# Polysketch attention and cosine router: queries in the keys' form, routing in pieces, ten early expert blocks

## The chip, the cores and the metric

One Trainium2 chip, one of its cores. The metric is the device time of one execution in microseconds (us). The engines are TensorE (PE in the views; PEld is its weight loads), VectorE (DVE), ScalarE (ACT), GpSimd (POOL) and SyncE (SP, which issues plain DMAs). SBUF is the working memory of 128 partitions; PSUM is where TensorE writes.

## The reference

Polynomial-sketch attention for 4 batches x 4 heads, 1088 positions of 32 numbers, then a router that sends each of 4352 tokens (128 numbers, the four heads side by side) to the best of 8 experts.

```python
phi(x) = outer(S1 @ x, S2 @ x).reshape(64)          # 8 x 8 features of a position
kv, z = sum_s phi(k_s) v_s^T, sum_s phi(k_s)
x = (phi(q) @ kv) / (phi(q) . z + 1e-6)             # 4 heads -> 128 numbers per token
logits = normed(x) @ normed(expert_emb).T / tau
e, g = argmax(logits), softmax(logits)[argmax]
out = g * (relu(x @ w1[e]) @ w2[e])                 # w1[e]: 128 x 1024, w2[e]: 1024 x 128
```

All inputs and the output are float32.

## The kernel before

The batches are handled in two halves (m = 0, 1) of two batches; a half has 17 tiles of 128 positions.

**Keys** (`k_steps`, L256): in groups of four tiles, `tr` transposes the tiles on TensorE, `ab` multiplies them with the block matrix `Sblk` (L270, 96 columns), ScalarE copies one sketch out, VectorE multiplies the two to features `kp` (L276), and `kv` adds up features times values over all tiles in PSUM (L288). At the end the sums go to `kz`, with a mask that keeps each head's own part.

**Queries** (`q_steps`, L311) have features across partitions: `fa` and `fb` multiply the transposed tiles with the expanded sketches `Sa` and `Sb` (L328, up to 512 columns, two passes for each of two head pairs), ScalarE copies one product and VectorE multiplies it with the other (L340). `nd` multiplies with `kz` (L348, weights of 64 columns, one half of the output's partitions at a time), VectorE divides (L354 to L356), `xt` transposes the result, ScalarE sums squares, `logit` multiplies with the embeddings (L372).

**Order.** `k_steps` and `q_steps` are lists of steps that `put` lays on ticks (L555 to L572): keys of m = 0 one group per tick, then keys of m = 1 with queries of m = 0, then queries of m = 1. A scheduler orders the instructions of these stages.

**Routing** (`pick` L379, `gate_tokens` L394, `route_and_run_experts` L413) comes after all logits: one-hot choices, two products that count them and rank them (L418, L419), a scan, slots, gates on all tokens (on GpSimd), one write per half of the gated tokens to the DRAM buffer `x_dram`, then a table from block and row to token, built with products of one-hot rows and columns (L454 to L470). From it come `src_i`, `dst_i` (token to gather, row to scatter) and `exp_i` (expert of each block).

**Expert blocks** (L542): 41 blocks of 128 tokens, in written order on VectorE and TensorE. Block i: `fetch(i + 4)` gathers tokens with an indirect DMA on GpSimd (L497), `up(i)` does 16 passes and a Relu on ScalarE (L522, L523), `turn(i + 1)` transposes the next tokens (L503, L505), `weights(i + 1)` copies the expert's matrices by a number that VectorE loads to a register (L512, L513), `down(i - 1)` does 16 passes, a copy on ScalarE (L531) and an indirect DMA that scatters to the output (L532). TensorE executes its queue in order.

Of the kernel before, what the change touches and what calls it, by code (L numbers as in the profile page):

```python
# [19 lines left out]
P = 128  # L20
# [13 lines left out]
K_GROUPS = ((0, 4), (4, 8), (8, 12), (12, 16), (16, 17))  # L34
Q_GROUPS = ((0, 4), (4, 8), (8, 11), (11, 14), (14, 17))
# [4 lines left out]
DIGIT = 128  # L40
AHEAD = 4
# [8 lines left out]
def kernel(  # L50
# [28 lines left out]
    def ps_acc(i):  # L79
        return psum.tile([P, 512], F32, tag=f"acc{i}", bufs=1, name=f"ps_acc{i}")  # L80
# [6 lines left out]
    def rows_tile(name):  # L87
        return rows_p.tile([P, NC, H, D], F32, tag="rows", name=name)

    def load_q(m):  # L90

        for i in range(2):
            for h in range(H):
                nc.sync.dma_start(
                    q_sb[m][i * HALF:(i + 1) * HALF, :, h],
                    bass.AP(tensor=q.tensor, offset=q.offset + ((2 * m + i) * H + h) * S * D,
                            ap=[[NC * D, HALF], [D, NC], [1, D]]))


    v_sb = [consts.tile([P, 6, NC, D], F32, name=f"v{m}") for m in range(NM)]  # L100

    def load_k(m, i):
        for h in range(H):
            nc.sync.dma_start(
                k_sb[m][:, i * NK:(i + 1) * NK, h],
                bass.AP(tensor=k.tensor, offset=k.offset + ((2 * m + i) * H + h) * S * D,
                        ap=[[NK * D, P], [D, NK], [1, D]]))

    def load_v(m, i):
        for p in range(2):  # L110
            nc.sync.dma_start(
                v_sb[m][:, 3 * p:3 * p + 2, i * NK:(i + 1) * NK],
                bass.AP(tensor=v.tensor, offset=v.offset + ((2 * m + i) * H + 2 * p) * S * D,
                        ap=[[NK * D, P], [S * D, 2], [1, NK * D]]))

    def load_rest(m):
        for i in range(2):
            r = slice(i * HALF, (i + 1) * HALF)
            at = (2 * m + i) * H * S * D + SK * D
            nc.sync.dma_start(k_sb[m][r, NC - 1],  # L120
                              bass.AP(tensor=k.tensor, offset=k.offset + at, ap=[[D, HALF], [S * D, H], [1, D]]))
            for p in range(2):
                nc.sync.dma_start(v_sb[m][r, 3 * p:3 * p + 2, NC - 1],
                                  bass.AP(tensor=v.tensor, offset=v.offset + at + 2 * p * S * D,
                                          ap=[[D, HALF], [S * D, 2], [1, D]]))
# [4 lines left out]
    for m in range(NM):  # L130
        k_sb[m] = rows_tile(f"k{m}")
        for i in range(2):
            load_k(m, i)
            load_v(m, i)
        load_rest(m)
        q_sb[m] = rows_tile(f"q{m}")
# [13 lines left out]
    for m in range(NM):  # L150
        for p in range(2):
            nc.gpsimd.memset(v_sb[m][:, 3 * p + 2], 1.0)

    mask4 = consts.tile([P, H], F32, name="mask4")
    maskh = consts.tile([P, 2], F32, name="maskh")
    for t in (mask4, maskh):
        nc.vector.memset(t, 0.0)
    for h in range(H):
        nc.vector.memset(mask4[h * D:(h + 1) * D, h:h + 1], 1.0)
    for h in range(2):  # L160
        nc.vector.memset(maskh[HALF * h:HALF * (h + 1), h:h + 1], 1.0)
# [40 lines left out]
    nc.gpsimd.memset(half_c, 0.5)
    x_dram = tc.dram_tile([N, DM], F32, name="x_dram")
# [8 lines left out]
    lane = iota([P, P], [[1, P]], 0, 0, "lane")  # L212
    part = iota([P, 1], [[1, 1]], 0, 1, "part")
    first = iota([P, E], [[-1, E]], E, 0, "first")
    start = iota([P, NT], [[P, NT]], 0, 0, "start")
# [7 lines left out]
    tok_d = consts.tile([P, 2, NT], F32, name="tok_d")  # L223
    nc.vector.tensor_copy(tok_d, tok_i[:, 1:])
    digits = [tok_d[:, d] for d in range(2)]
    before = consts.tile([P, P], F32, name="before")
    nc.vector.tensor_scalar(before, lane, part[:, 0:1], None, op0=ALU.is_gt)
    ones = consts.tile([P, P], F32, name="ones")
    nc.vector.memset(ones, 1.0)
    follows = consts.tile([P, E, NT], F32, name="follows")  # L230
    nc.vector.memset(follows, 1.0)
    nc.vector.memset(follows[:, :, 0:1], 0.0)

    enT = consts.tile([P, 96], F32, name="enT")
    nc.vector.memset(enT, 0.0)

    def prep_emb():
# [12 lines left out]
        nc.vector.tensor_copy(enT[:, :E], ps[:, :E])  # L250


    kz = {}
    acc = {}

    def k_steps(m, c0, c1):  # L256
# [3 lines left out]
        def tr():  # L260
            ps = ps_small()
            for j in range(n):
                nc.tensor.transpose(ps[:, j * P:(j + 1) * P], k_sb[m][:, c0 + j].rearrange("p h d -> p (h d)"), ident)
            s["kT"] = work.tile([P, 512], F32, tag="xT", name="kT")
            nc.scalar.copy(s["kT"][:, :n * P], ps[:, :n * P])

        def ab():
            ps = ps_small().rearrange("p (j g r) -> p j g r", j=4, r=2 * R)
            for j in range(n):
                nc.tensor.matmul(ps[:, j, :6], s["kT"][:, j * P:(j + 1) * P], Sblk, start=True, stop=True)  # L270
            b_sb = work.tile([P, 4, H, R], F32, tag="b", name="b_sb")
            nc.scalar.copy(b_sb[:, :n], ps[:, :n, :H, R:])  # L272
            s["kp"] = work.tile([P, 4, H, R, R], F32, tag="kp", name="kp")
            for j in range(n):
                a, b = ps[:, j, :H, :R], b_sb[:, j]
                nc.vector.tensor_mul(s["kp"][:, j],  # L276
                                     bview(a, [list(a.ap[1]), list(a.ap[2]), [0, R]]),
                                     bview(b, [list(b.ap[1]), [0, R], list(b.ap[2])]))

        def kv():  # L280
            if c0 == 0:
                acc[m] = [ps_acc(i)[:, :6 * D].rearrange("p (a n) -> p a n", a=2) for i in range(2)]
            for c in range(c0, c1):
                rest = c == NC - 1
                for i in range(2) if rest else (c // NK,):
                    r = slice(i * HALF, (i + 1) * HALF) if rest else slice(0, P)
                    for p in range(2):
                        nc.tensor.matmul(  # L288
                            acc[m][i][:, p],
                            s["kp"][r, c - c0, 2 * p:2 * p + 2].rearrange("s h i j -> s (h i j)"),  # L290
# [318 lines left out]
```

## Time and profile before

| what | us |
|---|---|
| median of 3 runs (307.32 to 312.07) | 307.79 |
| the profiled execution | 309.62 |
| its span, first to last instruction | 307.8 |
| TensorE busy / its weight loads | 254.5 / 230.3 |
| VectorE, ScalarE, GpSimd busy | 140.1, 86.5, 107.2 |

Times below are from the start of the profiled span. In a view, a line names the kernel's line (L522), the engine, the operation, what it writes and reads, shapes, a count, busy time or mean time, and in brackets or after a bar the idle time before it and what ended that. The granted clock is a share of 2.4 GHz: 1.00, or 0.50 for 1.2 GHz, or a mean of both.

### The profile page before, as it was taken

To read this page: it belongs to the slowest core of one execution; us is meant where nothing else is said; L and a number is where in the kernel's file an instruction comes from. 1 tells how busy PE (TensorE), PEld (TensorE's weight loads), DVE (VectorE), ACT (ScalarE), POOL (GpSimd) and SP (SyncE) were. 2 spreads that over 40 slices of the span, in tenths; PEclk is the share of its full clock that TensorE was granted. 3 is DMA by queue.
4 is the path that set the end of the run, shared out by engine and by line. 5 is a ranking of instruction groups with operands and counts; after the bars stand their busy time and mean duration, and the time that the engine had idled before them with its cause. 6 is when DMAs were issued, how large, how long until landed. Compare 5 with 4: busy or idle time off the path is not lost. (4 is left out here: it accounts for less than half of the span.)

```text
span 307.8 us, 5515 instructions
## 1 busy us (share of the span) xinstructions
PE 254.5 (83%) x2127; PEld 230.3 (75%) x2127; DVE 140.1 (46%) x345; ACT 86.5 (28%) x195; POOL 107.2 (35%) x103
## 2 busy tenths in 40 slices
PE   0987999999799750125999999999999999999960
PEld 0886777776467530114999999999999999999960
DVE  7334254345464448982344444444444444444400
ACT  1121242332245210001133333333333333333320
POOL 4000000000413034017455666555666556632230
PEclk9999799999999955555799999999999999999995
DMA  6999799993003001102111111111111111210000
GB/s 122 167 136 171 146 135 327 336 345 85 0 2 145 1 2 66 79 0 48 30 34 38 34 37 28 36 30 44 37 30 37 34 40 32 36 25 19 15 2 0
DMA packets 51194, 22.59 MB, mean 73 GB/s; under 512 B 38425, under 2 KB 48676, under 8 KB 50912
## 3 DMA queue, kind: packets, MB, share of 16 engines
q1 hardware_dynamic: 48544, 17.31, 24.2%
q0 software_dynamic: 2624, 4.92, 6.2%
q8 instruction: 17, 0.28, 0.4%
q14 instruction: 9, 0.07, 0.1%
HBM read 17.77 MB, written 4.92 MB: 74 GB/s over the span
## 5 line engine op out<-in xcount | busy, mean ns | idle before, releaser
L522 PE MATMUL ps_big<-xTb,w1b 128*128 128x128 f32 x656 | 83.6, 283 | 1.7 <-issue 1.3
L522 PEld LDWEIGHTS ps_big<-xTb,w1b 128*128 128x128 f32 x656 | 79.8, 199 | 2.4 <-issue 1.7
L529 PE MATMUL ps_acc<-w2b,hT 128*128 128x128 f32 x656 | 79.8, 275 | 0.0
L529 PEld LDWEIGHTS ps_acc<-w2b,hT 128*128 128x128 f32 x656 | 76.4, 192 | 0.0
L523 ACT ACTIVATE hT<-ps_big 128x1024 f32<-128x1024 f32 x41 | 42.1, 1027 | 94.6 <-PE ps_big L522 83.6
L497 POOL DMA_INDIRECT xs<-x_dram,src_i x41 | 48.0, 1170 | 39.4 <-PE ps_t L503 21.4
L532 POOL DMA_INDIRECT out_dram<-y,dst_i x41 | 41.4, 1010 | 50.3 <-ACT y L531 48.4
L505 DVE COPY xTb<-ps_t 128x128 f32<-128x128 f32 x41 | 12.0, 292 | 75.0 <-PE ps_t L503 75.0
L512 DVE COPY w1b<-w_sb 128x1024 f32 x41 | 28.5, 694 | 13.5 <-DVE xTb L505 12.1
L399 POOL TENSOR_TENSOR nrm<-ssq,half_c 128x17 f32<-128x17 f32 x2 | 6.2, 3087 | 65.7 <-ACT sq L367 65.7
L513 DVE COPY w2b<-w_sb 128x1024 f32 x41 | 28.5, 694 | 0.0
L340 DVE TENSOR_TENSOR qp<-a_sb,ps_big 128x768 f32<-128x768 f32 (+1 forms) x10 | 10.6, 1055 | 23.4 <-PE ps_big L328 20.3
L531 ACT COPY y<-ps_acc 128x128 f32<-128x128 f32 x41 | 11.0, 267 | 33.9 <-PE ps_acc L529 33.9
L288 PE MATMUL ps_acc<-v,kp 128*128 128x96 f32 (+1 forms) x144 | 19.8, 295 | 0.8 <-DVE kp L276 0.8
L288 PEld LDWEIGHTS ps_acc<-v,kp 128*128 128x128 f32 (+1 forms) x144 | 18.2, 206 | 2.9 <-DVE kp L276 1.6
L276 DVE TENSOR_TENSOR kp<-ps_t,b_sb 128x256 f32<-128x256 f32 x34 | 12.1, 418 | 14.5 <-ACT b_sb L272 14.5
L469 PE MATMUL ps_acc<-col,row 128*128 128x82 bf16 x34 | 3.0, 269 | 18.3 <-DVE row L466 18.3
L328 PE MATMUL ps_big<-qT,Sa 128*128 128x384 f32 (+1 forms) x40 | 17.3, 556 | 0.0
L367 ACT ACTIVATE sq<-x 128x128 f32<-128x128 f32 x34 | 10.3, 308 | 24.2 <-DVE x L356 24.2
L469 PEld LDWEIGHTS <-row 128*128 128x128 bf16 x34 | 2.3, 138 | 19.7 <-DVE row L466 19.7
L328 PE MATMUL ps_big<-qT,Sb 128*128 128x384 f32 (+1 forms) x40 | 16.5, 534 | 0.0
L503 PE MATMUL ps_t<-ident,xs 128*128 128x128 f32 x41 | 11.5, 281 | 4.2 <-DMA xs<-x_dram,src_i 4.2
(137 smaller groups left out, 220.3 us busy)
## 6 DMA issues: line engine op xcount, KB each, us to landing
w_sb<-in_moe_w_dram SPq DMA_DIRECT2D x16, 512.0 KB, 8.3
q<-in_q_dram SPq DMA_DIRECT2D x16, 136.0 KB, 4.2
x_dram<-x SPq DMA_DIRECT2D x2, 1088.0 KB
k<-in_k_dram SPq DMA_DIRECT2D x16, 128.0 KB, 3.8
v<-in_v_dram SPq DMA_DIRECT2D x8, 256.0 KB, 3.3
xs<-x_dram,src_i POOLq DMA_INDIRECT x41
out_dram<-y,dst_i POOLq DMA_INDIRECT x41
k<-in_k_dram SPq DMA_DIRECT2D x4, 32.0 KB, 3.4
```

The lines of the kernel that those rows point to most:

```text
L276: nc.vector.tensor_mul(s["kp"][:, j], bview(a, [list(a.ap[1]), list(a.ap[2]), [0, R]]), bview(b, [list(b.ap[1]), [0, R], list(b.ap[2])]))
L288: nc.tensor.matmul(acc[m][i][:, p], s["kp"][r, c - c0, 2 * p:2 * p + 2].rearrange("s h i j -> s (h i j)"), v_sb[m][r, 3 * p:3 * p + 3, c], ...
L328: nc.tensor.matmul(ps[:, p, :w], S_[:, 2 * p:2 * p + 2].rearrange("p h i j -> p (h i j)"), s["qT"][:, :w], start=True, stop=True)
L497: nc.gpsimd.indirect_dma_start(out=xs[i][:], out_offset=None, in_=x_dram[:, :], in_offset=bass.IndirectOffsetOnAxis(ap=src_i[:, i:i + 1], ...
L503: nc.tensor.transpose(ps[:, :P], xs.pop(i), ident)
L505: nc.vector.tensor_copy(xT[i], ps[:, :P])
L512: nc.vector.tensor_copy(w1b[i], w1_sb[:, bass.ds(e, 1)].rearrange("p o f -> p (o f)"))
L513: nc.vector.tensor_copy(w2b[i], w2_sb[:, bass.ds(e, 1)].rearrange("p o f d -> p (o f) d"))
L522: nc.tensor.matmul(ps[:, u, j * P:(j + 1) * P], w[:, f * P:(f + 1) * P], x, start=True, stop=True)
L523: nc.scalar.activation(hT[i], ps, ACT.Relu)
L529: nc.tensor.matmul(ps, h[:, f * P:(f + 1) * P], w[:, f], start=f == 0, stop=f == NF - 1)
L532: nc.gpsimd.indirect_dma_start(out=out[:, :], out_offset=bass.IndirectOffsetOnAxis(ap=dst_i[:, i:i + 1], axis=0), in_=y[:], in_offset=None ...
```

## The change

- Queries get features like keys, across the free axis (`turned`, `sketch`, `second`, `features` serve both), and are then transposed (`tr_qp`). k, q and v are loaded in larger pieces, one DMA per batch.
- Sketches, key sums and logits are done on halves of the output's partitions, with weights of 64 columns; the masks go.
- Routing is done per eight tiles (`router`: `pick`, `place`, `mark`), with a slot's block key being the expert's region of 64 keys. Logits and the reciprocal norm are written beside each token to DRAM rows of 137 numbers (`write`), and the gate is worked out per block (an Exp in `up`, `share` on VectorE, a scale in `down`'s copy).
- The table has two parts. `plan_early` and a table over the 17 tiles of m = 0 make 10 full blocks (`EARLY`), which gather from a copy of the rows of m = 0; `plan_late` and a table over all 34 tiles make the other 31.
- Every step has a tick and a rank in it. TensorE, VectorE, ScalarE and GpSimd keep that order. Blocks run one per tick from tick 31; the early ones stand beside the last queries' steps and the late table.

```diff
+    def sketch(ps, t, n):
+        for u in range(2):
+            r = slice(u * HALF, (u + 1) * HALF)
...
+                for h in range(H):
+                    nc.tensor.matmul(ps[r].rearrange("p (g h r) -> p g h r", h=H, r=2 * R)[:, :, h],
+                                     t[:, h * P + u * HALF:h * P + (u + 1) * HALF], Sblk, start=True, stop=True)
...
+    def features(ab, b, n, tag):
+        t = work.tile([P, 4, H, R * R], F32, tag=tag, name=tag)
+        nc.vector.tensor_mul(t[:, :n].rearrange("p j h (i k) -> p (j h) i k", i=R),
+                             ab[:, :, 0].unsqueeze(3).broadcast_to([P, n * H, R, R]),
+                             b[:, :n * H].unsqueeze(2).broadcast_to([P, n * H, R, R]))
...
+    def keys(m, c0, c1, put, late):
...
+        put(0, 60, tr)
+        put(1, 51, ab)
+        put(1, 61, b)
+        put(1, 63, prod)
+        put(5 if late else 3, 30, kv)
...
+    def queries(m, c0, c1, put):
...
+        put(0, 61, tr)
+        put(1, 50, ab)
+        put(1, 60, b)
+        put(1, 62, prod)
+        put(3, 10, tr_qp)
+        put(4, 20, nd)
+        put(5, 20, xt)
+        put(5, 80, squares)
+        put(6, 10, logit)
+        put(6, 70, best)
+        if c1 == NC or c1 % SPAN == 0:
+            pick, place, mark, store, write = router(m, c1 - at - n, c1)
+            put(5, 81, store)
+            put(6, 71, pick)
+            put(7, 40, place)
+            put(7, 90, mark)
+            put(7, 39, write)
...
+    def weights(i):
...
+        w2 = w2_sb[:, bass.ds(e, 1)].rearrange("p o f d -> p (o f) d")
+        if t == 0:
+            nc.scalar.copy(w2b[i], w2)
+        else:
+            nc.vector.tensor_copy(w2b[i], w2)
...
+    def up(i):
...
+        nc.scalar.activation(p, xs[i][:, DM:DM + E], ACT.Exp, scale=xs[i][:, ROW - 1:], accum_out=gate[i])
+
+    def share(i):
+        nc.vector.tensor_scalar_add(gate[i], gate[i], PROB_EPS)
+        nc.vector.reciprocal(gate[i], gate[i])
...
+    def block(i):
+        if i + AHEAD < EARLY or ready <= i + AHEAD < NBLK:
+            fetch(i + AHEAD)
+        if i < NBLK:
+            up(i)
+        if i + 1 < NBLK:
+            turn(i + 1)
+            weights(i + 1)
+        if i < NBLK:
+            share(i)
+        if i > 0:
+            down(i - 1)
...
     tick = 0
+    for g in GROUPS:
+        keys(0, *g, put_at(tick), True)
         tick += 2
+    put_at(tick)(0, 0, prep_emb)
+    for g in GROUPS:
+        keys(1, *g, put_at(tick), False)
+        queries(0, *g, put_at(tick))
         tick += 2
+    put_at(tick)(5, 50, plan_early)
+    for f in table(0, NC, lambda: early["key"]):
+        put_at(tick)(5, 91, f)
+    put_at(tick)(8, 90, first_block)
+    for g in GROUPS:
+        queries(1, *g, put_at(tick))
+        tick += 2
+    put_at(tick)(5, 50, plan_late)
+    steps = table(1, NT, lambda: late["key"])
+    for i, f in enumerate(steps):
+        put_at(tick)(5 + i, 95, f)
+    for i in range(NBLK + 1):
+        put_at(tick)(i + 1, 55, lambda i=i: block(i))
+    ready = 3 + len(steps) + AHEAD + 1
+    put_at(tick)(4 + len(steps), 96, lambda: [fetch(i) for i in range(EARLY, ready)])
```

## Rows read from the trace of the kernel before

**Rows 1.** Busy time by stretch, with granted clock, DMA share and GB/s.

```profile
0.00:30.00 30.00, 19.40 (x125) 17.68 (x125) 13.80 (x72) 5.35 (x13) 4.01 (x17) 1.00 0.89 148
30.00:72.00 42.00, 40.93 (x324) 31.19 (x324) 17.75 (x42) 13.47 (x43) 0.00 (x0) 0.96 1.02 254
72.00:110.00 38.00, 33.44 (x293) 23.42 (x289) 18.75 (x53) 14.30 (x57) 7.74 (x3) 0.99 0.08 31
110.00:146.00 36.00, 9.76 (x57) 7.26 (x56) 26.38 (x60) 1.10 (x2) 12.89 (x9) 0.50 0.12 41
146.00:297.60 151.60, 150.91 (x1335) 150.74 (x1335) 63.46 (x119) 51.99 (x81) 81.59 (x75) 0.99 0.12 32
297.60:307.80 10.20, 0.01 (x1) 0.00 (x0) 0.00 (x0) 0.27 (x1) 0.98 (x1) 0.64 0.00 0
```

**Rows 2.** Timeline, two starts of the block loop's transposes (start us, us, what).

```profile
168.56 0.14 PEld L503 LDWEIGHTS ps_t<-ident,xs 128*128 128x128 f32 x1
...
172.25 0.14 PEld L503 LDWEIGHTS ps_t<-ident,xs 128*128 128x128 f32 x1
```

**Rows 3.** Groups by form: four instructions of the block loop.

```profile
L523 ACT ACTIVATE hT<-ps_big 128x1024 f32<-128x1024 f32 x41 | 42.1, 1027 | 94.6 <-PE ps_big L522 83.6 <-issue 11.1
...
L531 ACT COPY y<-ps_acc 128x128 f32<-128x128 f32 x41 | 11.0, 267 | 33.9 <-PE ps_acc L529 33.9
...
L512 DVE COPY w1b<-w_sb 128x1024 f32 x41 | 28.5, 694 | 13.5 <-DVE xTb L505 12.1 <-DVE exp_i L490 0.9 <-issue 0.4
...
L497 POOL DMA_INDIRECT xs<-x_dram,src_i x41 | 48.0, 1170 | 39.4 <-PE ps_t L503 21.4 <-DVE pad L480 16.2 <-issue 1.2
```

**Rows 4.** Timeline, weight loads and products of TensorE in the attention part.

```profile
7.34 1.09 PE L263 MATMUL ps_t<-ident,k 128*128 128x128 f32 x4 [1.46 <-DMA k<-in_k_dram]
...
9.10 1.78 PEld L270 LDWEIGHTS ps_t<-Sblk,kT 128*128 128x128 f32 x8 [1.08 <-ACT kT L265]
...
30.12 0.42 PEld L263 LDWEIGHTS ps_t<-ident,k 128*128 128x128 f32 x4
...
42.62 1.91 PE L328 MATMUL ps_big<-qT,Sa 128*128 128x512 f32 x4
...
44.69 1.86 PEld L288 LDWEIGHTS ps_acc<-v,kp 128*128 128x128 f32 x16
...
50.64 1.07 PEld L348 LDWEIGHTS ps_big<-kz,qp 128*64 128x64 f32 x32
...
51.78 0.97 PEld L270 LDWEIGHTS ps_t<-Sblk,kT 128*128 128x128 f32 x8
```

**Rows 5.** Groups by form: VectorE operations.

```profile
L340 DVE TENSOR_TENSOR qp<-a_sb,ps_big 128x1024 f32<-128x1024 f32 x4 | 4.8, 1206 | 9.5 <-PE ps_big L328 9.5
...
L466 DVE TENSOR_TENSOR row<-lane_b,blk_row 128x1152 bf16<-128x1152 bf16 x3 | 4.1, 1353 | 0.0
...
L356 DVE TENSOR_TENSOR x<-ps_big,rc 128x512 f32<-128x512 f32 x4 | 2.8, 692 | 0.2
...
L386 DVE TENSOR_SCALAR lt<-lg 128x136 f32<-128x136 f32 x2 | 0.5, 227 | 0.0
```

**Rows 6.** Timeline, first and last step of the embeddings' chain.

```profile
25.98 0.30 ACT L241 ACTIVATE emb_sq<-emb_sb 8x128 f32<-8x128 f32 x1
...
29.92 0.20 PE L249 MATMUL ps_t<-ident,emb_sq 8*128 8x8 f32 x1 [1.57 <-DVE emb_sq L247]
```

**Rows 7.** Timeline, first gather and the transposition that waits for it.

```profile
137.39 1.50 POOL L497 DMA_INDIRECT xs<-x_dram,src_i  x1 [16.18 <-DVE pad L480]
...
140.56 0.45 PE L503 MATMUL ps_t<-ident,xs 128*128 128x128 f32 x1 [4.17 <-DMA xs<-x_dram,src_i]
```

**Rows 8.** Busy time in two short stretches (columns as in rows 1).

```profile
32.00:34.00 2.00, 2.00 (x9) 1.72 (x9) 0.33 (x2) 0.27 (x1) 0.00 (x0) 0.50 1.01 202
...
108.00:110.00 2.00, 1.43 (x9) 1.07 (x7) 0.00 (x0) 1.12 (x7) 0.80 (x1) 0.82 0.00 0
```

**Rows 9.** Groups by form: loads of ScalarE's tables.

```profile
L265 ACT ACT_TABLE_LOAD x1 | 1.3, 1283 | 0.7 <-PEq L593 0.7
```

More of the change, by code (lines that the diff above doesn't have):

```diff
@@ L100 @@
[L100 to L114 removed]
+            r = slice(i * HALF, (i + 1) * HALF)
@@ L260, in tr, with ab, b, prod @@
         def tr():
[L261 to L278, printed above, removed]
+            s["kT"] = turned(None if n == 1 else k_sb[m][:, :, c0 // NK, c0 % NK:c0 % NK + 4], k_rest[m], n, "kT")
+        def ab(ps):
+            s["ab"] = sketch(ps[:, 256:], s["kT"], n)
+        def b():
+            s["b"] = second(s["ab"], n, "kb")
+        def prod():
+            s["kp"] = features(s["ab"], s["b"], n, "kp")
         def kv():
             if c0 == 0:
-                acc[m] = [ps_acc(i)[:, :6 * D].rearrange("p (a n) -> p a n", a=2) for i in range(2)]
+                acc[m] = ps_one("acc")[:, :8 * D].rearrange("p (i a n) -> p i a n", i=2, a=2)
+            end = ps_small()[:, :4 * D].rearrange("p (a n) -> p a n", a=2) if c1 == NC else None
             for c in range(c0, c1):
@@ new lines, in logit, with best @@
+                for u in range(2):
+                    r = slice(u * HALF, (u + 1) * HALF)
+                    nc.tensor.matmul(ps[r, j], s["xT"][:, j * P + u * HALF:j * P + (u + 1) * HALF], enT,
+                                     start=True, stop=True)
+            s["lg"] = work.tile([P, 4, E], F32, tag="lg", name="lg")
+            nc.scalar.copy(s["lg"][:, :n], ps[:, :n])
+        def best():
+            mx = work.tile([P, 4], F32, tag="mx", name="mx")
+            nc.vector.reduce_max(out=mx[:, :n], in_=s["lg"][:, :n], axis=AX.X)
+            nc.vector.tensor_sub(xg[g][:, own, DM:DM + E], s["lg"][:, :n],
+                                 mx[:, :n].unsqueeze(2).broadcast_to([P, n, E]))
@@ new lines, in plan_late @@
+    def plan_late():
+        ps = ps_small()[:, :E]
+        nc.tensor.matmul(ps, ones, counts[0], start=True, stop=True)
+        took = early["took"]
+        ni, all_, left, upto, t = column("n_late", I32), column("all"), column("left"), column("upto1"), column("steps")
+        nc.vector.scalar_tensor_tensor(out=ni, in0=ps, scalar=float(P - 1), in1=region, op0=ALU.add, op1=ALU.subtract)
+        nc.vector.tensor_scalar(ni, ni, 7, None, op0=ALU.logical_shift_right)
+        nc.vector.tensor_copy(all_, ni)
+        nc.vector.tensor_sub(left, all_, took)
+        nc.vector.tensor_tensor_scan(out=upto[:], data0=ones[:, :E], data1=left[:], initial=0.0, op0=ALU.mult, op1=ALU.add)
+        nc.vector.tensor_sub(t[:, :E - 1], took[:, 1:], all_[:, :E - 1])
+        nc.vector.tensor_scalar_add(w_late[:, :E - 1], t[:, :E - 1], float(KEYS))
+        at = blocks(1, upto, w_late)
+        nc.vector.scalar_tensor_tensor(out=at, in0=at, scalar=took[:, 0:1], in1=lane[:, :LATE], op0=ALU.add, op1=ALU.add)
+        late["key"] = at
```

557 lines of the change are left out of this document (290 added, 267 removed).

## Prediction

> **What bounds the kernel now.** I read the stretches first [rows 1]. There are four parts: keys of the first half alone (0 to 30 us), keys of the second half beside queries of the first (30 to 72), queries of the second half (72 to 110), and the expert blocks (146 to 297.6), with a gap from 110 to 146 and a tail of 10.2 us. In the blocks TensorE is busy for 150.9 of 151.6 us: one block starts 3.69 us after the other [rows 2], and ScalarE, VectorE and GpSimd fit under it [rows 3]. From 30 to 72 TensorE is full too (40.9 of 42). In the gap VectorE works 26.4 of 36 us and TensorE 9.8, at the low clock (0.50, the 1.2 GHz level). So what can be had is the gap, where only VectorE's routing chain runs, and TensorE's work before it.
>
> Then the pace of single instructions [rows 4]. A weight load of 128 columns with its product takes 0.121 us at the high clock (8 in 0.97), 0.116 for the key sums (16 in 1.86), a transposition 0.105 (4 in 0.42), and one on 64 columns, the form that the change spreads, 0.0335 (32 in 1.07). The first loads after the start are slow: 8 in 1.78 us.
>
> **The change, part by part.** I sum by the ticks of the new order: A (ticks 0 to 10, keys 0), B (10 to 19, keys 1 and queries 0), C (20 to 30, queries 1) and D (from the first block in tick 31). A float32 product is two passes.
>
> A. The loads: pieces of 1 to 2.2 KB instead of 128 bytes, one DMA where there were four. The first transposition waits for them until 7.34 now [rows 4]; I take 6.3 (bounds 5.5 and 7.3: before it stands VectorE's chain on the sketch, or nothing changes). Per group of four tiles the sketch is 16 narrow passes (0.5 us, at the slow start twice that, 1.1), then ScalarE's copy (0.27 [rows 3]) and one feature product of 1024 elements, 1.21 us [rows 5] (bounds 1.0, the pace of ScalarE's 1024 elements [rows 3], and 1.35, that of 1152 [rows 5]). The sketch has a single PSUM buffer, so these follow each other: 2.8 us with the handovers. First transpositions and copy to 8.1, four groups 11.2, the small one and the key sums that don't fit under it 1.7: A ends at 21.0. Then TensorE's queue has the embeddings' transposition at its head, and behind it all of B; from ScalarE's square to it took 3.9 us [rows 6], part of it waiting on VectorE for key sums that now come later; I take 2.5 (bounds 1.5 and 3.9). B starts at 23.5.
>
> B is TensorE's. Transpositions: 34 of tiles, 32 of features, 12 of results, 78 at 0.105 = 8.2 us. Narrow passes: sketches 34 tiles x 4, key sums 20 tiles x 8 and 16 for the remainder, numerators 12 x 8, logits 8 x 4, together 440 at 0.0335 = 14.7. With the ranks 23.1 us. What goes is the wide feature product, 1.91 us for half of a group of four [rows 4], so 3.8 per group. VectorE has 18 us in B (eight full feature products 9.7, three divisions 3.6, some 20 small ones 4.6) and ScalarE no more, one tick apart, so they hide; filling the new pipeline in ticks 10 to 13, where a feature product stands between sketch and transposition, costs 2.5 (bounds 0 and 5). The clock: after the pause before the embeddings' transposition now (1.57 us idle [rows 6]) the products of 32 to 34 run at 0.50 [rows 8]; the pause stays, and I take 2.0 (bounds 0 and 4). B is 27.6 and ends at 51.1.
>
> C is VectorE's, TensorE waits in it. Feature products 6.0 (one per group, and those of the small groups); the division of the numerators, 0.69 for the large step [rows 5] and 1.2 with the two before it, 5.4 over five groups; marks 2.7 at the pace of the 1152-element row [rows 5]; three small products of the early table 1.1; the first block's copies 1.0 [rows 3]. The rest is small operations at 0.23 [rows 5]: 33 in three routings, 10 in the maxima, 28 in the reciprocals, the sums, the early plan and table, 71 in all, 16.3. Sum 32.5. TensorE's sum here is 18.1: 68 transpositions 7.1, 288 narrow passes 9.7, the early table's 17 products 1.3, taken between a narrow pass and a transposition. Two waits are VectorE's too: for the 17 products of the early table, which stand behind the tick's other products (1.4), and for block 0. Its gather is behind the power on GpSimd in tick 27, and takes 3.2 us to the transposition now [rows 7]; the transposition stands in tick 28 on TensorE, with the next queries behind it and VectorE's copy behind that: 2.0 exposed (bounds 0 and 3.2). From the last numerators to the first block's product 1.7. C is 37.6 and ends at 88.7. The scattered writes of rows instead of one per half go by SP's queue, which has nothing else then.
>
> D. Gating moves from GpSimd to a scale in ScalarE's last copy and costs nothing there: per block 1.03 + 0.27 [rows 3] plus an Exp (taken as two of the 0.27 row) is under 3.69 even with the 1.03 us copy of one weight matrix in early blocks (2.87 in all; the load of the expert's number on ScalarE, which no row shows, is free up to the other 0.8 and costs ten times the rest beyond it). A gather of 548 bytes a row for 512 is taken at the same 1.17 [rows 3]; GpSimd has over a microsecond left in each block. VectorE has 0.7 to 1.4 [rows 3] and three small ones. So 41 blocks are 41 x 3.69 = 151.3. Added on TensorE: the late table's 34 products, 3.0 (3.6 at a transposition's pace), and 1.5 of the last two groups' remains: 4.5. Added waits, all behind VectorE: the ranks of ticks 33 and 35 stand ahead of a block's products on TensorE and wait for the picks, which VectorE does after the block's copies (1.4 and 1.2); in tick 35 ranks, late plan and table begin before the copies for the next block (1.7). 4.3 in all (bounds 0 and 8). The gap hands the clock over at 0.50 now [rows 1]; C has fewer and shorter pauses, and I take 2.0 (bounds 0 and one block's 3.7). D is 162.1 and ends at 250.8. The tail stays 10.2 [rows 1]: 261.0.
>
> The profiled execution took 309.62 us with a span of 307.8, and the median of the runs shown is 307.79; a span thus stands for the median as it is. Forecast: 261.0.
>
> Where the trace says least is the clock in C. From 108 to 110 TensorE was busy 1.43 of 2 us in pieces and fell (0.82 over these 2 us, 0.50 after) [rows 8]. In C it would work 18.1 of 37.6 us. The Trainium skill, "TensorE: Matmul & The Clock Gate", section "HAM oscillation — how this bites in real kernels", says that bursts of products with waits between them go back to the slow clock at each wait; the trace agrees as far as rows 8 go, and by it the second rival below would be the case. On the other hand, the Trainium skill, "TensorEngine Tiling (Array Packing)", section "Key Properties", says that a change of tiling mode drains the engine, which speaks against many short narrow stretches. The trace disagrees: the 32 narrow loads from 50.64 end at 51.71 and the next wide load begins at 51.78 [rows 4], 0.07 us later.
>
> **The rivals.** First, the waits are covered: the hand-made order lets VectorE run ahead so that none of 1.4, 2.0 and 4.3 shows, the fill (2.5) goes, and the clock stays up (4.0). 261.0 - 14.2 = 246.8. For it speaks that no engine is over 90% by my sums in C; against it, that every engine keeps its written order.
>
> Second, the clock stays low in C. TensorE's 18.1 become 36.2, and in ticks without routing it then sets the pace: 5 more; B stays cold twice as long (2), the first blocks run slow as now (2). 270.
>
> Third, the narrow passes don't overlap as the numerators' do, since the sketch does all of one half before the other: half of a full load, 0.06 each. B gains 440 x 0.0265 = 11.7; A and C hide it: 272.7. Against it is only one row of such passes [rows 4], with another order of halves.
>
> Fourth, the change doesn't do what it says: block 0 starts only when the late table is done, because a gather waits for writes that it doesn't need. Ticks 30 to 38 then hold some 20 us of VectorE's chain, of which 8.8 are in D already: 272.
>
> Fifth, slower: ScalarE loads a table at each change between Relu, Exp and Copy in the block loop. One load is 1.28 us [rows 9]. With three per block, late blocks take 1.84 + 3.84 = 5.7 and early ones 6.7: 31 x 2.0 + 10 x 3.0 = 92 us more, 353. It decides from 5.0 us of ScalarE per block (47 us and 2% over 41 blocks). Against it: the kernel uses these functions now and the trace has a single load.
>
> **How the numbers follow.** Forecast 0.45 (its own range 251 to 270), first rival 0.23, second and third together 0.22, fourth 0.06, fifth 0.02, and 0.02 that several terms are wrong by so much that nothing is left. A measurement of this kernel can tell 2% (6 us) from no change. The range takes in the first four: 243 to 278. Faster 0.96, within 2% 0.02, slower 0.02.
>
> **What would show it.** Right: the first up-product near 89 us, blocks 3.7 us apart from then on, no stretch without TensorE longer than 4 us after 24; TensorE nearly full from 24 to 51 and VectorE from 51 to 89; numerators and sketches at 0.03 to 0.04 a pass. Wrong: a first block past 100 us (fourth rival, or VectorE's small operations dearer than 0.23), a granted clock of 0.50 through C (second), sketches at 0.06 (third), blocks further apart than 3.8 us (fifth), or a first block before 78 (first).

## Result and profile after

The changed kernel took 282.46 us (median of 4 runs, 280.29 to 285.32) beside 307.87 for the kernel before: a ratio of 0.916 (95%: 0.907 to 0.925). It is faster by 8%, but 21 us behind the forecast of 261.0 and outside its range (243 to 278). Its first profiled execution was one with a lowered clock (285.32 us), so the trace read here is that of the same kernel run again: 280.74 us, span 278.9. In that second measurement the median was 285.12 (280.74 to 285.51).

Busy time by stretch, with the columns and clock of [rows 1]; the stretches are cut at the steps of the forecast: B, C, D's early blocks, its late ones. In a line stand the stretch, its length, the busy time of TensorE, its weight loads, VectorE, ScalarE and GpSimd (instructions in brackets), the granted clock, the DMA share and GB/s.

```profile
22.60:55.05 32.45, 26.28 (x537) 23.77 (x538) 16.36 (x36) 15.08 (x46) 1.68 (x1) 1.00 1.07 307
55.05:103.07 48.02, 32.68 (x425) 28.93 (x423) 30.17 (x111) 18.47 (x71) 8.81 (x8) 0.75 0.17 60
103.07:130.00 26.93, 21.41 (x173) 20.24 (x173) 12.56 (x58) 12.76 (x34) 9.59 (x9) 0.87 0.13 42
130.00:268.70 138.70, 137.23 (x1250) 136.73 (x1249) 69.49 (x192) 65.68 (x154) 76.14 (x69) 1.00 0.14 32
```

| step | forecast | in the trace | miss |
|---|---|---|---|
| B starts (embeddings' transposition) | 23.5 | 22.6 | -0.9 |
| B, to the numerators of tick 20 | 27.6 | 32.4 (to 55.05) | +4.8 |
| C, to the first up-product | 37.6 | 48.0 (to 103.07) | +10.4 |
| D, to TensorE's last product | 162.1 | 165.6 (to 268.65) | +3.5 |
| tail | 10.2 | 10.2 | 0 |

The misses add up to 17.9 (from unrounded times), which is 278.9 less 261.0. In B TensorE is busy for 26.3 us where 23.1 were counted, and idle for 6.2 where 2.5 were allowed for the fill; the 2.0 allowed for the clock were not needed in this execution (1.00). In C VectorE is busy for 30.2 us (forecast 32.5): its work was counted well, and what was not counted is its idle time, 17.8 us in place of 5.1. TensorE is slow there (0.75) and busy 32.7 us where 18.1 were forecast.

The block loop is as forecast. Timeline, two starts of late blocks' transpositions: 3.69 us apart, as in [rows 2].

```profile
161.69 0.14 PEld L611 LDWEIGHTS ps_t<-ident,xs 128*128 128x128 f32 x1
...
165.38 0.14 PEld L611 LDWEIGHTS ps_t<-ident,xs 128*128 128x128 f32 x1
```

Groups by form: a feature product, a division, the new Exp, GpSimd's power, and ScalarE's one table load.

```profile
L642 ACT ACTIVATE probs<-xs 128x8 f32<-128x8 f32 x41 | 12.0, 292 | 0.0
...
L291 DVE TENSOR_TENSOR qp<-ps_ab,qb 128x1024 f32<-128x1024 f32 x8 | 9.8, 1224 | 17.6 <-ACT kb L286 13.7 <-ACT qb L286 3.8
...
L493 POOL TENSOR_TENSOR xg<-ssq,half_c 128x8 f32<-128x8 f32 x4 | 6.7, 1666 | 71.6 <-ACT lg L415 71.6
...
L391 DVE TENSOR_TENSOR xg<-ps_big,rc 128x512 f32<-128x512 f32 x8 | 5.5, 691 | 0.3
...
L269 ACT ACT_TABLE_LOAD x1 | 1.3, 1283 | 0.7 <-PEq L742 0.7
```

Where the waits are. First TensorE's own (engine, what it was to write, whom it waited for: us in all, times, longest), then VectorE's for GpSimd.

```profile
PE ps_t L397 <- DVE mx L419: 6.2, 4, 2.1
...
PE ps_t L611 <- DMA xs<-rows,src_i: 5.1, 1, 5.1
PE ps_t L550 <- DVE col L545: 3.9, 1, 3.9
PE ps_t L471 <- DVE oh L460: 3.0, 2, 2.1
PE ps_t L397 <- DVE xg L391: 2.8, 3, 1.2
PE ps_t L253 <- DVE emb_sq L251: 2.2, 1, 2.2
PE ps_t L471 <- DVE oh L458: 1.7, 1, 1.7
```

```profile
DVE xg L494 <- POOL xg L493: 10.7, 5, 3.5
```

Of the five waits 0.6 us lie in B, 3.4 in C and 6.8 in D. One of them in VectorE's timeline, at the end of tick 17, and two later ones: the two steps of `store` (L494, L495) wait for the power, and behind them, in the written order, stand tick 18's division and, on TensorE, the transposition of its result in tick 19.

```profile
49.11 1.21 DVE L291 TENSOR_TENSOR kp<-ps_ab,kb 128x1024 f32<-128x1024 f32 x1
50.91 0.17 DVE L494 TENSOR_SCALAR xg<-xg 128x8 f32<-128x8 f32 x1 [0.58 <-POOL xg L493]
...
51.24 0.13 DVE L389 TENSOR_SCALAR rc<-ps_big 128x16 f32<-128x16 f32 x1
...
63.86 0.17 DVE L494 TENSOR_SCALAR xg<-xg 128x8 f32<-128x8 f32 x1 [1.68 <-POOL xg L493]
...
111.93 0.17 DVE L494 TENSOR_SCALAR xg<-xg 128x8 f32<-128x8 f32 x1 [3.52 <-POOL xg L493]
```

Last, TensorE's timeline around block 0: 5.08 us without work for the first gather, and then a granted clock of 0.50 until 106.5 us. The first 16 up-products take 3.62 us, the next 2.02.

```profile
94.20 0.45 PE L611 MATMUL ps_t<-ident,xs 128*128 128x128 f32 x1 [5.08 <-DMA xs<-rows,src_i]
...
103.07 3.62 PE L637 MATMUL ps_big<-xTb,w1b 128*128 128x128 f32 x16
...
108.18 2.02 PE L637 MATMUL ps_big<-xTb,w1b 128*128 128x128 f32 x16 [0.51 <-DVE w1b L623]
```

### The profile page after: what moved, and what is told of

It is laid out like the page before. It is cut to its first block, busy times and chain, and to the rows that moved or that the text cites. A ratio compares the mean times of both kernels' runs of the same rounds, so it can differ in the third digit from the quotient of the medians.

```text
span 283.5 us, 6567 instructions
## 1 busy us (share of the span) xinstructions
PE 237.2 (84%) x2558; PEld 226.7 (80%) x2558; DVE 139.4 (49%) x444; ACT 117.9 (42%) x315; POOL 101.2 (36%) x105
## 5 line engine op out<-in xcount | busy, mean ns | idle before, releaser
L605 POOL DMA_INDIRECT xs<-rows,src_i x41 | 47.9, 1168 | 12.6 <-PE ps_t L611 7.8
L652 PE MATMUL ps_acc<-w2b,hT 128*128 128x128 f32 x336 | 41.0, 275 | 0.0
L652 PE MATMUL ps_ab<-w2b,hT 128*128 128x128 f32 x320 | 40.0, 280 | 0.0
L652 PEld LDWEIGHTS ps_acc<-w2b,hT 128*128 128x128 f32 x336 | 39.2, 192 | 0.0
L652 PEld LDWEIGHTS ps_ab<-w2b,hT 128*128 128x128 f32 x320 | 38.5, 197 | 0.0
L291 DVE TENSOR_TENSOR qp<-ps_ab,qb 128x1024 f32<-128x1024 f32 (+1 forms) x10 | 10.6, 1062 | 20.3 <-ACT kb L286 16.4
L611 PE MATMUL ps_t<-ident,xs 128*128 128x128 f32 x41 | 11.7, 285 | 4.9 <-DMA xs<-rows,src_i 4.9
L383 PE MATMUL ps_big<-kz,qpT 128*64 128x66 f32 x272 | 14.7, 270 | 0.0
L383 PEld LDWEIGHTS ps_big<-kz,qpT 128*64 128x64 f32 x272 | 13.5, 178 | 0.0
L327 PE MATMUL ps_acc<-v,kp 128*64 128x64 f32 (+1 forms) x272 | 12.3, 255 | 1.2 <-DVE kz L336 1.2
L327 PEld LDWEIGHTS ps_acc<-v,kp 128*64 128x64 f32 (+1 forms) x272 | 10.8, 164 | 3.1 <-issue 2.6
```

The costliest lines, as they stand in the source:

```text
L291: nc.vector.tensor_mul(t[:, :n].rearrange("p j h (i k) -> p (j h) i k", i=R), ab[:, :, 0].unsqueeze(3).broadcast_to([P, n * H, R, R]), b[: ...
L327: nc.tensor.matmul(own[u * HALF:(u + 1) * HALF, p], s["kp"][r, c - c0, h], bass.AP(tensor=vo.tensor, offset=vo.offset, ap=[list(vo.ap[0]), ...
L383: nc.tensor.matmul(ps[i * HALF:(i + 1) * HALF, j, p * W:(p + 1) * W], s["qpT"][:, p, j * P + i * HALF:j * P + (i + 1) * HALF], kz[m][:, i, ...
L605: nc.gpsimd.indirect_dma_start(out=xs[i][:], out_offset=None, in_=rows[t][:, :], in_offset=bass.IndirectOffsetOnAxis(ap=src_i[t][:, j:j + ...
L611: nc.tensor.transpose(ps[:, :P], xs[i][:, :DM], ident)
L652: nc.tensor.matmul(ps, h[:, f * P:(f + 1) * P], w[:, f], start=f == 0, stop=f == NF - 1)
```

## Experiments

Four theories for the 18 to 21 us: VectorE stands behind GpSimd's power (P); single waits of TensorE, for the early table and the gather, cost their length (W); TensorE's clock, low behind such waits, costs more than they do (K); the narrow passes are dearer than counted (N). Each measurement has its own runs of the kernel before, whose median went from 307.9 to 311.6 us, so ratios with their intervals are compared. One kernel measured twice (e10, e16) gave 0.852 and 0.871, so less than 0.02 (6 us) between two measurements settles nothing by itself. The measurement of e0, e6, e7 and e8 was too uneven for a verdict against the kernel before; e6, e7 and e8 are set against each other. Expected were 279 to 283 us for e0 and 264 to 268 for e16; both medians came out above. The last column has the lengths of B, C and D in the profiled execution, cut as above.

| run | edit | median (range) us | ratio (95%) | first up-product | span | B, C, D |
|---|---|---|---|---|---|---|
| e0 | none | 285.12 (280.74 to 285.51) | 0.929 (0.922 to 0.937) | 103.1 | 278.9 | 32.4, 48.0, 165.6 |
| e1 | `store`'s end later | 270.73 (269.34 to 273.93) | 0.872 (0.864 to 0.879) | 98.1 | 267.6 | 31.6, 43.6, 159.3 |
| e2 | gathers earlier | 281.91 (277.38 to 283.7) | 0.900 (0.889 to 0.910) | 101.0 | 278.5 | 32.5, 46.1, 167.2 |
| e3 | idle transpositions | 277.08 (273.62 to 277.99) | 0.890 (0.881 to 0.899) | 97.4 | 271.7 | 32.4, 42.5, 164.0 |
| e4 | no early blocks | 292.55 (291.09 to 295.19) | 0.944 (0.936 to 0.952) | 125.6 | 290.5 | 33.8, 68.3, 154.6 |
| e5 | e1, wide sketches, logits | 281.67 (277.1 to 282.39) | 0.903 (0.894 to 0.911) | 108.6 | 278.1 | 41.2, 43.7, 159.2 |
| e6 | e1 + e2 | 270.41 (268.73 to 271.15) | 0.881 (0.868 to 0.894) | 96.2 | 267.7 | 31.5, 41.9, 161.3 |
| e7 | e6 + e3 | 267.87 (265.72 to 269.2) | 0.872 (0.857 to 0.887) | 96.5 | 266.1 | 33.1, 39.9, 159.2 |
| e8 | e6, early table later | 268.29 (268.15 to 268.65) | 0.874 (0.867 to 0.881) | 95.6 | 266.6 | 34.2, 38.0, 160.7 |
| e9 | e8, `store`'s end still later | 266.82 (264.79 to 270.11) | 0.862 (0.857 to 0.867) | 91.8 | 263.9 | 31.5, 37.7, 161.8 |
| e10 | e9, key sums first | 265.60 (262.07 to 268.07) | 0.852 (0.845 to 0.859) | 88.7 | 262.4 | 29.9, 35.9, 163.5 |
| e11 | e1, halves in turn | 270.75 (267.95 to 272.43) | 0.872 (0.866 to 0.877) | 99.0 | 270.4 | 32.6, 45.0, 161.1 |
| e12 | e10 + e11 | 265.56 (264.71 to 267.27) | 0.859 (0.853 to 0.864) | 90.9 | 263.7 | 29.8, 38.9, 162.5 |
| e13 | e12 + idle transpositions | 269.53 (267.82 to 272.24) | 0.873 (0.867 to 0.879) | 93.4 | 265.8 | 29.3, 42.7, 162.1 |
| e14 | idle transpositions at the embeddings | 282.35 (280.93 to 284.16) | 0.913 (0.907 to 0.919) | 103.6 | 279.5 | 33.7, 47.0, 165.6 |
| e15 | e10 + idle transpositions | 268.16 (265.14 to 270.54) | 0.866 (0.861 to 0.871) | 92.1 | 265.0 | 29.8, 38.7, 162.6 |
| e16 | e10 again | 268.61 (266.18 to 270.58) | 0.871 (0.867 to 0.875) | 91.5 | 264.3 | 29.8, 39.2, 162.6 |

**P: the power.** e1 leaves the power where it is and moves VectorE's two steps behind the pick.

```diff
             put(5, 81, store)
+            put(6, 75, norm)
             put(6, 71, pick)
...
+        def norm():
+            d = xg[m, c0 // SPAN][:, :n, ROW - 1]
             nc.vector.tensor_scalar_add(d, d, NORM_EPS)
             nc.vector.reciprocal(d, d)
```

> The two VectorE steps after GpSimd's power go behind the division, the maxima and the picks of the next tick. In the changed kernel's trace VectorE waits for the power five times, 11.1 us in all, and TensorE idles about 9 us there. Waits theory (the excess over the forecast is queues waiting for GpSimd): 6 to 10 us faster, 273 to 277 us, no VectorE wait for the power. Clock theory (a pause costs mostly through the low clock after it): 9 to 14 us faster, with the stretches after 56 and 72 us at the high clock. Sum theory (VectorE simply has more work between the last keys and the first block than forecast): 0 to 3 us.

The ratio falls from 0.916 to 0.872, the intervals apart: 11.7 us by the medians. VectorE's two steps no longer wait for the power anywhere. B is 0.9 us shorter, C 4.5 and D 6.3, which follows the 0.6, 3.4 and 6.8 us that VectorE had waited there. The sum lies above the 6 to 10 us of the theory of waits and inside the 9 to 14 of the clock theory; the clock rose too, from 0.87 to 1.00 over the early blocks, and what it has of the 11.7 us was not separated. Busy time of e1 by the same stretches (54.5, 98.05 and 257.4 are the same steps):

```profile
22.90:54.50 31.60, 26.29 (x539) 23.79 (x539) 16.31 (x36) 15.07 (x46) 1.68 (x1) 1.00 1.05 297
54.50:98.05 43.55, 29.43 (x425) 25.95 (x422) 30.30 (x111) 18.54 (x71) 8.89 (x8) 0.80 0.22 78
98.05:130.00 31.95, 27.88 (x261) 26.74 (x260) 21.75 (x79) 19.60 (x48) 13.14 (x12) 1.00 0.14 42
130.00:257.40 127.40, 127.36 (x1163) 127.02 (x1162) 60.74 (x171) 58.45 (x139) 73.13 (x66) 1.00 0.14 34
```

**W: the gather.** e2 puts the first four gathers ahead of the power, at tick 26.

```diff
-    def first_block():
+    def first_fetch():
         for i in range(AHEAD):
             fetch(i)
+
+    def first_block():
...
+    put_at(tick)(6, 95, first_fetch)
     put_at(tick)(8, 90, first_block)
```

> The first four gathers go ahead of the next power on GpSimd, two ticks earlier. TensorE now waits 4.9 us for the first gather and then runs at half clock from 98.7 to 111 us. Waits theory: the 4.9 us go and nothing else, 277 to 279. Clock theory: the slow 12 us go too, 6 more, 270 to 274. Sum theory: VectorE is late anyway, 280 to 283.

The pause of 5.08 goes, but the first up-product comes only 2.1 us earlier, D is 1.6 us longer, and the ratio's interval overlaps that of the unaltered kernel (0.907 to 0.925). With the power's wait gone it is no better:

> The late steps of store (as in e1) and the four gathers at tick 26 (as in e2) together; the pause of 4.5 us before the early table's products stays. Theory of the waits (what a pause costs is its own length): the gather's pause, 4.6 us in e1, goes, so 265 to 267 us, first up-product at 93 to 94. Theory of the clock (what follows a pause runs at half pace): besides the pause the slow stretch behind it goes, so 261 to 264. Theory that the gathers are hidden anyway: 270, as e1.

270.4, as e1: C is 1.6 us shorter and D 2.0 longer. In e6's timeline of TensorE the wait for the gather (4.57 us in e1) is gone, but the ranks (L472, a product of `place`) wait 2.76 us for VectorE's copy of block 0's tokens, since they write to the buffer which that copy frees. On VectorE that copy stands behind the picks and the copy of a weight matrix; there is no wait for the power. Block 0's up-products then take 3.62 us, where they take 1.95 in e1; the granted clock from 90 to 100 us is 0.50 in e6 and 0.83 in e1. Timeline of e6, two lines, then of e1:

```profile
90.34 0.21 PE L472 MATMUL ps_t<-oh,before 128*128 128x64 bf16 x1 [2.76 <-DVE xTb L617]
...
96.15 3.62 PE L641 MATMUL ps_big<-xTb,w1b 128*128 128x128 f32 x16
```

```profile
98.05 1.95 PE L641 MATMUL ps_big<-xTb,w1b 128*128 128x128 f32 x16
```

In e8, which adds the edit of the next part to e6, the gathers come later, and the power stands on GpSimd right behind the four of them. Timelines of GpSimd and VectorE: VectorE's moved step waits 1.13 us for the power, and behind that stand block 0's copies.

```profile
85.07 0.95 POOL L609 DMA_INDIRECT xs<-rows,src_i  x1 [0.30 <-issue]
86.05 1.69 POOL L494 TENSOR_TENSOR xg<-ssq,half_c 128x8 f32<-128x8 f32 x1
```

```profile
87.78 0.17 DVE L498 TENSOR_SCALAR xg<-xg 128x8 f32<-128x8 f32 x1 [1.13 <-POOL xg L494]
...
88.81 0.69 DVE L627 COPY w1b<-w_sb 128x1024 f32 x1 [0.62 <-DVE xg L499]
89.42 0.28 DVE L617 COPY xTb<-ps_t 128x128 f32<-128x128 f32 x1
```

The ranks on TensorE wait 4.06 us for that last copy. e9 moves the step and the write one tick on, for the second half alone.

```profile
89.76 0.21 PE L472 MATMUL ps_t<-oh,before 128*128 128x64 bf16 x1 [4.06 <-DVE xTb L617]
```

> e8 with the late steps of store and the write one tick later for the second half alone, because in e6 and e8 the power stood on GpSimd behind the four gathers and VectorE waited 1.1 us for it with the placing behind. Theory that the gain of the early gathers was given back by this wait: first up-product 1 to 3 us earlier than in e8 (95.6), 265 to 267.5. Theory that TensorE's wait of 4.1 us there is VectorE's own sum: within 1 us of e8, 268.

The first up-product comes 3.7 us earlier than in e8, and the expectation seems to hold; but the two traces part long before the edit's place. In e8's the clock fell behind the wait for the embeddings (0.52 from 23 to 30 us, 1.00 in e9's), B starts 0.7 us later and is 2.7 longer. C, in which the edit acts, takes 38.0 us in e8 and 37.7 in e9. That the gain of the early gathers was given back by the wait for the power is thus not shown.

Busy time from 23.2 to 30 us, in e8, then in e9:

```profile
23.20:30.00 6.80, 6.61 (x76) 6.14 (x77) 0.30 (x2) 1.37 (x4) 0.00 (x0) 0.52 1.04 214
```

```profile
23.20:30.00 6.80, 5.65 (x103) 4.87 (x101) 2.64 (x3) 3.34 (x7) 0.00 (x0) 1.00 1.09 221
```

**W: the early table.** e8 moves the early table's products from tick 25 to 26.

```diff
-    for f in table(0, NC, lambda: early["key"]):
-        put_at(tick)(5, 91, f)
+    for i, f in enumerate(table(0, NC, lambda: early["key"])):
+        put_at(tick)(5 if i < 3 else 6, 91, f)
```

> e6 with the early table's products one tick later (tick 26 in place of 25), so that TensorE does not stand and wait for VectorE's chain of the early plan. Theory that the pause of 4.5 us there is TensorE's loss: 3 to 6 us below e6, the pause before the early table's products gone. Theory that VectorE's sum sets this stretch whatever TensorE waits for: within 1 us of e6, with the same idle time of TensorE in other places.

The pause ahead of the products falls from 4.49 to 0.96, that ahead of the ranks rises from 2.76 to 4.06, and the median falls by 2.1 us, with overlapping intervals. C falls by 3.9 us, but B is 2.7 longer in e8's execution, at the low clock. e9, which has this edit too and B as in e6 (31.5), has the first up-product 4.3 us earlier than e6 and a median 3.6 lower, in another measurement. So the early table's products a tick later are worth some 2 to 4 us. That stays an estimate: two executions of one kernel (e10, e16) differ by 3.3 us in C.

**K: the clock.** e3 adds idle transpositions and takes no wait away.

```diff
-            ps = ps_small()[:, :2 * n]
+            full = ps_small()
+            ps = full[:, :2 * n]
+            for _ in range(36 if which == 0 else 0):
+                nc.tensor.transpose(full[:, :P], ident, ident)
...
+        for _ in range(44 if i == 0 else 0):
+            nc.tensor.transpose(ps[:, :P], ident, ident)
```

> No wait is taken away. 36 idle transpositions of the identity stand before the early table's products and 44 before the first block's transposition, so that TensorE works during the two longest pauses (3.8 and 4.9 us). Clock theory: the stretches from 84.5 to 91 and from 98.7 to 111 run at the high clock, 6 to 9 us faster, 273 to 276. Waits theory and sum theory: no gain, 281 to 285.

The granted clock is 1.00 from 72 to 100 us, where it was 0.80 and 0.64, C is 5.5 us shorter and D 1.6, and the ratio falls to 0.890 against 0.916. Each of e3's four runs is below each of the ten of the unaltered kernel: added work made the kernel faster. So K holds in the changed kernel, for some 5 us. Busy time of the unaltered kernel (e0), then of e3:

```profile
72.00:90.00 18.00, 12.41 (x174) 11.08 (x172) 9.80 (x43) 6.99 (x26) 1.22 (x1) 0.80 0.03 9
90.00:100.00 10.00, 5.59 (x56) 5.28 (x58) 6.35 (x22) 3.87 (x13) 5.39 (x6) 0.64 0.32 94
```

```profile
72.00:90.00 18.00, 16.98 (x245) 15.82 (x244) 11.94 (x53) 7.94 (x27) 3.72 (x3) 1.00 0.05 14
90.00:100.00 10.00, 8.28 (x120) 7.36 (x120) 5.89 (x19) 4.39 (x15) 2.91 (x4) 1.00 0.29 86
```

With the waits for the power and the gather gone, less of it shows in the time:

> e6 and the idle transpositions of e3 ahead of the early table's products and of block 0's transposition; they take no wait away. Theory of the clock: the stretch behind the one pause that is left runs at full pace, 3 to 6 us below e6. Theory of the waits alone: the same as e6 within 1 us, or up to 2 us above it, since the added work comes after the gather's wait has gone.

2.5 us at the medians, overlapping intervals. C and D together are 4.1 us shorter than in e6, and B, where the clock fell to 0.75 from 23 to 30 us in this execution, is 1.6 longer.

> e10 with 20 idle transpositions in each of three places where they wait for nothing: the embeddings' wait, ahead of the early table's products, and ahead of block 0's transposition. Theory of the clock: the clock stays at 1.00 behind the first two, and blocks 0 and 1 (3.62 and 3.50 us in e10 where a warm one takes 2.0) lose less: 1 to 4 us below e10 in the same call. Theory that only the waits are left: the same as e10, or 1 to 2 above it for the transpositions themselves.

No difference from e10 in the same measurement (e16, 268.61). But the added transpositions did not keep the clock up ahead of block 0: from 90 to 96 us it is 0.59, and the first up-products take 3.30 us, so this run settles less than it was meant to.

```profile
92.07 3.30 PE L648 MATMUL ps_big<-xTb,w1b 128*128 128x128 f32 x16
```

e13 put such transpositions ahead of the ranks, in place of those ahead of block 0:

> e12 with idle transpositions in the three pauses that are left: 20 in the embeddings' wait, 20 ahead of the early table's products, 22 ahead of the ranks of the second half's first eight tiles. They take no wait away. Theory that the rest above the forecast of 261.0 is the low clock behind these pauses: 3 to 5 us below e12, granted clock 0.97 or more over the whole span. Theory that it is the waits: the same as e12.

It lost 4.0 against e12. In the trace those 22 waited for the buffer themselves and then ran on the path at a granted clock of 0.50; C is 3.8 us longer:

```profile
83.65 4.96 PE L475 MATMUL ps_t<-ident 128*128 128x128 f32 x22 [2.35 <-DVE xTb L627]
```

> The changed kernel with 20 idle transpositions ahead of the embeddings' transposition, in its wait of 2.2 us; no wait is taken away. Theory that the changed kernel's times lie at 280 or at 285 because the clock falls behind this wait in some executions and not in others (0.54 over 24 to 30 us in one profile, 1.00 in another): no execution above 282, median 279 to 281, clock 1.00 from 23 to 52. Rival, that the scatter has its cause elsewhere: 280 to 285 as before.

The clock is 1.00 from 23 to 52 us, and yet three of six runs lie above 282, up to 284.16, and the median is that of the first measurement (282.46). The theory fails by its own forecast, and keeping the clock up behind that one wait shows no gain. The range is narrower than the unaltered kernel's (280.29 to 285.51), so it is not excluded that a part of the scatter came from there.

**N: the narrow passes.** e5 is e1 with whole weights in `sketch` and `logit`, e11 is e1 with `for h` outside and `for u` inside in `sketch`.

> e1 with the sketches and the logits back on whole weights of 128 columns (8 passes where there are 16). From rows 4 a sketch of four tiles then takes 0.97 us; in the trace of the changed kernel it takes 0.83 alone and 0.65 beside the other one of its tick, and 16 narrow logit passes take 0.55. If TensorE's passes lie on the path in ticks 10 to 20: 0.3 a sketch and 0.3 for logits over four groups, 2 to 4 us above e1. If the waits on VectorE set the pace there: within 1 us of e1.

10.9 us slower than e1, far more than expected, and in the traces 9.6 of it lie in B. Part is the passes: a pair of sketches takes about 2.0 us (48 to 50 us) and logits 0.94, against some 1.3 and 0.5. Part is the clock, which in e5 fell behind the same 2.2 us wait for the embeddings and did not in e1 (the granted clock is 0.64 against 1.00 from 30 to 52 us). How much each has was not separated.

> e1 with each sketch's halves in turn (half 0 and half 1 of one head's weights, then the next head) where all of one half came before the other. Theory that two loads on different halves overlap and two on the same don't: a sketch alone goes from 0.83 to about 0.55 us (16 at 0.034) and the pair of a tick from 1.3 to 1.1; in keys of the first half four times 0.3, later four times 0.2: 1 to 2 us below e1 where TensorE is on the path, none where it is not. Rival, that a sketch pass costs what its 64-column product costs whatever the order: no change in any of the three.

Timeline of e1, then of e11, in keys of the first half: the first sketch, slow as TensorE's first products were before [rows 4], and the last full one.

```profile
7.49 1.60 PE L280 MATMUL ps_ab<-Sblk,kT 128*64 128x64 f32 x16 [0.68 <-ACT kT L269]
...
17.73 0.94 PE L280 MATMUL ps_ab<-Sblk,kT 128*64 128x64 f32 x16
```

```profile
7.51 1.12 PE L280 MATMUL ps_ab<-Sblk,kT 128*64 128x64 f32 x16 [0.67 <-ACT kT L269]
...
16.47 0.69 PE L280 MATMUL ps_ab<-Sblk,kT 128*64 128x64 f32 x16
```

Sixteen passes go from 0.94 to 0.69 us, a fourth less, but the time stays: 270.75, beside 270.73 for e1. What else is in B stands in one tick's chain, which e10 changes:

```diff
-        put(5 if late else 3, 30, kv)
+        put(5 if late else 3, 30 if late or c0 == 0 else 15, kv)
```

> e9 with the key sums of the second half's groups 1 to 4 ahead of the transposition of the division's result, which waits 0.8 to 1.2 us for a division that stands on VectorE behind both feature products. Theory that these waits are part of what the stretch from 23 to 57 us took beyond the forecast: they go in three or four ticks, 3 to 4 us below e9. Theory that VectorE's or ScalarE's steps behind the transposition set the tick: within 1 us of e9.

In the trace TensorE's waits of 1.22, 0.79 and 1.13 us for the division are gone, and B takes 29.9 us against 31.5 in e9; it is 29.8 in e12, e15 and e16 too, which have the same edit. So B gains 1.6 us, less than the 3 to 4 expected. The time does not resolve it: e10 gave 265.60 once and 268.61 in e16. The first of these waits, in e9, and the same step in e10:

```profile
37.37 0.63 PE L397 MATMUL ps_t<-ident,xg 128*128 128x128 f32 x4 [1.22 <-DVE xg L391]
```

```profile
37.71 0.63 PE L397 MATMUL ps_t<-ident,xg 128*128 128x128 f32 x4
```

> All edits that paid together: e10 with the halves in turn of e11. Theory that TensorE's passes are on the path from 30 to 52 us once the transposition no longer waits: 0.3 for each of four pairs of sketches and 0.3 for each of five single ones, 1 to 2 us below e10 (265.6). Theory that VectorE sets the pace by then: no change from e10.

265.56. e9, e10 and e12 cannot be told apart; each beats both kernels, the changed one by 5 to 6%.

**The early blocks.** e4 puts every block eight ticks later, so that none stands beside queries or the late table.

```diff
-        put_at(tick)(i + 1, 55, lambda i=i: block(i))
+        put_at(tick)(i + 9, 55, lambda i=i: block(i))
...
```

> All blocks stand eight ticks later, behind the late table, so no early block runs beside the last queries' steps and the late table. All theories: slower; TensorE's own work there is 4.5 us and the rest is VectorE's. If the early blocks hide VectorE's ticks 31 to 38 as forecast, 11 to 18 us slower, 293 to 300; if they hide little, because both wait on the same VectorE queue, under 6 us.

10.1 us slower than the changed kernel, intervals apart (0.936 to 0.952, 0.907 to 0.925), and each of its runs above each of the ten of that kernel. It lies just below the 11 to 18 us expected if the early blocks hide VectorE's steps as forecast: starting blocks early is worth about 10 of the 25 us gained, the work of 2.7 blocks at 3.69.

## Why the prediction was wrong

Right were: A and the embeddings' wait (B starts 0.9 early), the sizes (feature products 1.22, division 0.69, copies and blocks, the tail), VectorE's sum in C, and that gating hides. Of the rivals, the fourth and fifth are out: there is one table load, and block 0 runs at 103 while the late table's products come at 144. The first, covered waits, went the other way. Of the signs of being wrong, a first block past 100 us came true, though for neither of the two causes named with it: VectorE's operations in C took less than counted.

What failed, in the order of its price:

- **"Two waits are VectorE's too."** The step counted who waits behind VectorE, and the power only as something ahead of the gather on GpSimd. That VectorE itself waits for the power, with the next division and so TensorE's transposition behind it, was in no term: it is 10.7 us of VectorE's waits in five places, and 11.7 us of the time (e1), with what the clock has of it. The order could be read from the change: `store` follows ScalarE's squares at a tick's end, goes through GpSimd and returns to VectorE ahead of the next tick's steps.
- **"the clock ... I take 2.0"**, twice. The clock fell behind the pauses and was 0.75 over C and 0.87 over the first blocks. Keeping it up was worth some 5 us (e3: 5.5 less in C and 1.6 in D), where 4.0 had been allowed for B and D, and nothing for C in the forecast. In B the 2.0 were not needed in e0's execution; in e8's they were (0.52 from 23 to 30 us, B 2.7 longer than in e9). The second rival had it at 270 with a chance of 0.22 shared; its mechanism was there, beside a larger one.
- **"2.0 exposed" for the gather, "1.4" for the early table.** The pauses were 5.1 and 3.9. Taking the first away gave nothing (e6 beside e1): what C gained, D lost, with block 0 at a clock of 0.50. Taking most of the second away gave some 2 to 4 us (e8, e9). So the gather's term was not too small for what could be had, and the early table's may have been by up to 2.5 us.
- **"filling the new pipeline ... costs 2.5".** B's waits do not end with the fill: in ticks 15 and 17 the transposition waits 1.2 and 0.8 us for a division that stands behind two feature products, in tick 19 2.1 with the power's wait in it, and one wait of 1.2 is for `kz`. TensorE idled 6.2 us there. B took 32.4, and 29.9 with the power's steps moved and the key sums ahead (e10).
- **The narrow passes at 0.0335.** Numerators and key sums run at it (32 in 1.19 and 1.15), sketches do not: 16 in 0.94 alone, 0.06 each, and a tick's 32 in some 1.3; with the halves in turn 16 take 0.69 (e11). TensorE was busy 26.3 us in B for 23.1 counted. The third rival was half right for these, and what e11 took off showed in no time. In C TensorE's 18.1 were too few as well: 25.8 even in e10, at a granted clock of 0.93.
- D's added work was counted too dear: the late table's 34 products took 1.18 us for 3.0. With the power's waits gone D took 159.3 (e1), less than the 162.1 forecast.

With P and what was tried of W and of B's waits, e10's profiled span is 262.4, within 2 us of the forecast, with B 29.9, C 35.9 and D 163.5; e16, the same kernel, has 264.3 with C 39.2. By medians (265.60 and 268.61) 5 to 8 us stay. That the sum then comes so near is partly luck: B and D are still over their terms, and C is under its own. Without the wait that had no term the time was 270.7 (e1), inside the range. Left open: how the 11.7 us of e1 divide between the waits and the clock behind them, what the clock still costs once these waits are gone, since in e15 it fell again ahead of block 0, and what the 3.3 us between e10 and e16 in C are.

## What to carry to other kernels

When an order is written by hand, list for each step that goes through another engine who stands behind its return, on the engine that gets the result; a step of 1.7 us on GpSimd, made a few times, cost 11.7 us here through the two 0.2 us steps on VectorE behind it. A pause in a row of waits is not yet a gain of its length: the gather's 4.6 us in e1 gave nothing, as the next wait was VectorE's. Two traces are compared step by step, from the first step at which they differ: e8 and e9 had parted before the edit acted. Adding idle work to keep the clock up is a quick test of what a pause costs beyond its length, if the trace shows that the clock did stay up (e15) and that the added work does not wait itself (e13).

## What was not expected of the hardware

TensorE's records show products of one group between those of another: in the timeline of the changed kernel, logits start between the sketch's last passes, 0.03 to 0.05 us apart in these lines. With the halves in turn (e11) each sketch's 16 stand together. In the records, then, the written order of TensorE's queue does not hold to the single pass, though a step that waits does hold up what is written behind it, as the transposition at 94.20 above.

```profile
47.08 0.22 PE L412 MATMUL ps_t<-enT,xT 128*64 128x8 f32 x1
47.13 0.22 PE L280 MATMUL ps_ab<-Sblk,kT 128*64 128x64 f32 x1
47.16 0.20 PE L412 MATMUL ps_t<-enT,xT 128*64 128x8 f32 x1
47.19 0.22 PE L280 MATMUL ps_ab<-Sblk,kT 128*64 128x64 f32 x1
```

Sixteen sketch passes took 0.94 us with all of one half first and 0.69 with the halves in turn. And 80 added transpositions (4.15 and 4.97 us of TensorE) made the kernel 5 us faster.
